# Float64 weights converted in place, and the second network's weights on GpSimd's DMA queue

## The chip, the cores and the metric

The kernel runs on one core of one Trainium2 chip. The core has a matrix engine (TensorE, PE in the profile, with its weight loads as PEld), a vector engine (VectorE, DVE), a scalar engine (ScalarE, ACT), GpSimd (POOL) and SyncE (SP), which here only issues transfers. The metric is the device time of one execution in microseconds, as the median of several runs; lower is better.

## The reference

Attention between 8 batches of 512 tokens and 32 state vectors for each of 8 heads, then two feed-forward networks on the 4352 rows that come out. All weights arrive as float64; `x` and `state` are float32, and so is the output.

```python
# x: (8, 8, 512, 64), state: (8, 8, 32, 64)
scores = scale * x @ state^T;  a  = softmax(scores);   xread = a @ state
scores2 = scale * state @ x^T; a2 = softmax(scores2);  sread = a2 @ x
x = concat([xread, sread], axis=2)      # -> rows of 512, (8 * 544, 512)
h = maximum(x @ w_in, 0)                # w_in (512, 2048)
x = (h * h) @ w_out                     # w_out (2048, 512)
a = x @ w1; b = x @ w2                  # (512, 1024) each
out = ((a * b) @ w3) @ w_out2           # w3 (1024, 1024), w_out2 (1024, 512)
```

## The kernel before

**Number format.** The kernel multiplies float32 values as pairs: `split` writes a rounded high half (a ScalarE cast, line 84) and the rest (a VectorE subtraction, line 85), and each product runs as three matmuls, high by high, low by high and high by low.

**Weights.** A float64 tile of 128x512 is loaded as pairs of int32 words (`load64`, lines 119 and 121, into a `raw` tile; there are 3 of them, and the `x` loads of lines 222 and 247 take the same ones). `convert64` makes float32 of it: `exponents` masks the exponent of the high word on VectorE (line 128) and rescales it on ScalarE (line 129); VectorE masks the mantissa (line 146), adds the low word (149), puts the sign to the exponent (152) and multiplies both (155). That is five VectorE instructions and one of ScalarE for each of 72 tiles.

**First network.** `h_tile(c, f)` makes 128 hidden features of chunk `c` (a batch; chunk 8 is the 256 state rows) in 6 matmuls, `act_h` squares the positive part and splits it into `ghl`, and `y_tile`, two tiles later, adds 12 matmuls with `w_out`'s halves into four PSUM banks (line 494). The hidden tiles need `SW`, a state times `w_in` (`make_sw`, line 426). The tiles run in a written order; `side[i]` and `late[i]` hold the attention steps and `conv()` calls that go beside tile `i`, held back behind an earlier tile's instruction by `issue_after`. A list `convs` has the order of the conversions: `w_out`'s first three tiles, `w_in`'s and `w_out`'s others, then 40 tiles of the second network (`later`: 8 of `w_out2`, 16 of `w3`, 16 of `w1` and `w2`). Each `conv()` converts one tile and starts the load of the one three places on. A `later` tile is stored as float32 in a DRAM scratch (line 214) and read back when the second network begins. Every transfer is issued by SyncE. Within these rules a scheduler sets the order on each engine when the kernel is built, and each engine then works through its list in order.

**Start.** Chunk 0 must have its attention and the first columns of `w_in` (`make_win0`, two halves by two) before its tiles run; columns 256 to 511 (`make_win0(1, 0)` and `(1, 1)`) come with tile 0, then `make_sw` for them, and tiles 2 and 3 wait for it.

**Between the networks.** `w3 @ w_out2` is multiplied out once: `load_wo2` and `load_w3` (line 641) bring the scratch back into `wst2` tiles, `w3_xpose` turns a 128x1024 row block of `w3` by 8 transposes on TensorE (line 692) into a PSUM bank, and splits it into `w3T`; `w34_rows` (line 707) multiplies it with `w_out2`'s halves in 24 matmuls. There are 8 row blocks. Beside that, `make_w` (lines 742 to 770) and `make_pair` (line 784) prepare the operands of the second network, whose matmuls (`quad`, `ab9`, `out_tile`) fill the rest of the time.

## Time and profile before

| what | value |
|---|---|
| median of 3 runs | 1258.58 us (1257.23 to 1260.12) |
| profiled execution, its own time | 1257.84 us |
| span of that execution's instructions | 1256.1 us |
| mean granted TensorE clock | 0.999 |
| instructions | 17499 |
| busy: PE, DVE, ACT, POOL | 1235.1, 789.0, 659.3, 33.5 us |
| moved by DMA | 143.23 MB, mean 114 GB/s |

Durations in the rows come from the one profiled execution, whose own time is 0.74 us under the median. A start-to-start distance of two instructions of an engine can be less than the duration shown, because the next one begins before the end of the last is recorded.

### The profile page before, as it was taken

Reading aid. Unit: us, or ns where it says so; the run is one execution under the profiler, and the core shown is the slowest. Engines: PE = TensorE matmul, PEld = TensorE weight load, DVE = VectorE, ACT = ScalarE, POOL = GpSimd, SP = SyncE. Lnnn points to the kernel's source line nnn. Section 1 sums busy time; section 2 is a strip of 40 time slices with the busy share of each in tenths; the row PEclk is TensorE's granted clock in tenths of the full one; section 3 lists DMA queues with packets and bytes.
Section 4 is the critical chain, followed back from the end, with each engine's and each line's share of the span. In section 5 each row is a group of like instructions: output and inputs, shape, how many; then the busy total and the mean of one; then the engine's idle time right before and its main releaser. Section 6 shows DMA issues by size and latency. Waiting matters only on the chain.

```text
span 1256.1 us, 17499 instructions
## 1 busy us (share of the span) xinstructions
PE 1235.1 (98%) x6672; PEld 982.1 (78%) x6672; DVE 789.0 (63%) x1403; ACT 659.3 (52%) x1188; POOL 33.5 (3%) x30
## 2 busy tenths in 40 slices
PE   6999999999999999999999999999999999999998
PEld 4667777777777777777799888888888888887886
DVE  6998778677585867742435835555655647474753
ACT  5687768666575756645655434444443524242430
POOL 0000000000000000000000000001500010000000
PEclk9999999999999999999999999999999999999999
DMA  6264646462634535201313520313430521423213
GB/s 218 69 207 145 173 129 201 113 184 82 156 130 86 190 76 173 89 18 34 134 42 111 201 76 9 120 48 126 143 134 9 201 76 52 149 74 128 76 59 117
DMA packets 125268, 143.23 MB, mean 114 GB/s; under 512 B 71680, under 2 KB 75264, under 8 KB 124672
## 3 DMA queue, kind: packets, MB, share of 16 engines
q1 hardware_dynamic: 125184, 142.11, 36.5%
q8 instruction: 52, 0.85, 0.3%
q14 instruction: 32, 0.26, 0.1%
HBM read 96.47 MB, written 45.61 MB: 113 GB/s over the span
## 4 chain that ended last, share of the span: by engine, by line
PE 93%; DMA 2%; ACT 2%; DVE 2%; issue 1%; SPq 0%; ACTq 0%; DVEq 0%
PE y L494 29%; PE po L903 14%; PE qa L822 10%; PE qd L822 7%; PE qc L822 3%; PE ps_w L707 3%; PE qe L822 3%; PE ps_sw L426 3%; PE ab L877 2%; DMA x<-in_x_dram 1%; PE ps_w L692 1%; PE ps_a L364 1%; PE ps_r L372 0%; PE ps_s L295 0%; DMA out_dram<-o 0%
## 5 line engine op out<-in xcount | busy, mean ns | idle before, releaser
L494 PE MATMUL y<-ghl,wo 128*128 128x512 f32 (+1 forms) x1728 | 403.0, 381 | 0.6 <-ACT wo L84 0.5
L494 PEld LDWEIGHTS y<-ghl,wo 128*128 128x128 f32 x1728 | 309.1, 188 | 88.4 <-ACT r L442 12.6
L85 DVE TENSOR_TENSOR ghl<-r,ghl 128x512 fp32r<-128x512 f32 (+1 forms) x144 | 95.0, 660 | 170.1 <-ACT ghl L84 167.4
L822 PE MATMUL qa<-yq,wq 128*128 128x512 f32 x576 | 146.3, 390 | 1.4 <-ACT s L830 1.4
L830 ACT COPY s<-qa 128x512 f32<-128x512 f32 x96 | 56.2, 589 | 143.7 <-PE qa L822 131.2
L822 PEld LDWEIGHTS qa<-yq,wq 128*128 128x128 f32 x576 | 107.5, 188 | 25.5 <-ACT s L830 2.4
L822 PE MATMUL qd<-yq,wq 128*128 128x512 f32 x384 | 98.4, 390 | 0.0
L903 PE MATMUL po<-w34b,c 128*128 128x512 f32 x408 | 95.8, 391 | 0.3 <-DVE o L912 0.3
L903 PE MATMUL po<-w,c 128*128 128x512 f32 x408 | 95.5, 391 | 0.0
L903 PEld LDWEIGHTS po<-w34b,c 128*128 128x128 f32 x408 | 75.7, 188 | 18.0 <-DVE c L85 1.0
L903 PEld LDWEIGHTS po<-w,c 128*128 128x128 f32 x408 | 75.5, 188 | 17.7 <-ACT o L909 1.1
L444 ACT ACTIVATE r<-r 128x512 f32<-128x512 f32 (+1 forms) x144 | 87.5, 608 | 2.9
L84 ACT CAST ghl<-r 128x512 fp32r<-128x512 f32 (+1 forms) x144 | 86.0, 597 | 3.5
L822 PEld LDWEIGHTS qd<-yq,wq 128*128 128x128 f32 x384 | 71.8, 188 | 15.7 <-ACT s L830 0.9
L129 ACT ACTIVATE ce<-ce,ebias 128x512 int32<-128x512 int32 x72 | 52.3, 727 | 44.3 <-DVE ce L128 44.3
L834 DVE TENSOR_TENSOR s<-qa,s 128x512 f32<-128x512 f32 x32 | 22.1, 692 | 75.0 <-ACT s L830 75.0
L780 POOL TENSOR_TENSOR yraw<-yraw,yp 128x512 f32<-128x512 f32 x24 | 32.8, 1373 | 987.9 <-DMA yraw<-yscr 815.2
L84 ACT CAST c<-s 128x512 fp32r<-128x512 f32 x64 | 39.7, 622 | 37.1 <-DVE s L851 36.1
L84 ACT CAST yq<-yraw 128x512 fp32r<-128x512 f32 x70 | 42.6, 622 | 24.1 <-DVE yraw L797 15.5
L912 DVE TENSOR_TENSOR o<-po,opart 128x512 f32<-128x512 f32 x34 | 23.3, 689 | 47.1 <-PE po L903 37.6
L152 DVE SCALAR_TENSOR_TENSOR ce<-raw,ce 128x512 int32<-128x512 int32 x72 | 49.3, 685 | 1.7 <-ACT ce L129 1.7
L85 DVE TENSOR_TENSOR yq<-yraw,yq 128x512 fp32r<-128x512 f32 x70 | 46.8, 684 | 5.0 <-ACT yq L84 4.7
(551 smaller groups left out, 1806.6 us busy)
## 6 DMA issues: line engine op xcount, KB each, us to landing
raw<-in_moe_w_dram SPq DMA_DIRECT2D x32, 512.0 KB, 4.3
yraw<-yscr SPq DMA_DIRECT2D x56, 256.0 KB, 5.5
yscr<-yo SPq DMA_DIRECT2D x52, 256.0 KB, 2.6
raw<-in_moe_w_out_dram SPq DMA_DIRECT2D x24, 512.0 KB, 3.9
oscr<-o SPq DMA_DIRECT2D x34, 256.0 KB, 2.2
opart<-oscr SPq DMA_DIRECT2D x34, 256.0 KB, 2.9
out_dram<-o SPq DMA_DIRECT2D x32, 256.0 KB, 2.9
raw<-in_moe_w_in_dram SPq DMA_DIRECT2D x12, 512.0 KB, 3.9
```

The source lines that it names most:

```text
L84: nc.scalar.copy(hi, src)
L85: return nc.vector.tensor_tensor(out=lo, in0=src, in1=f32(hi), op=ALU.subtract)
L129: nc.scalar.activation(e, e, ACTF.Relu, bias=ebias, scale=8.0)
L152: nc.vector.scalar_tensor_tensor(out=e, in0=hw, scalar=-(2**31), in1=e, op0=ALU.bitwise_and, op1=ALU.bitwise_or)
L426: mm = nc.tensor.matmul(pss[r][k * NS:(k + 1) * NS, cols], stT[rows, b, k, :], win_t[fg][rows, k, cols], start=True, stop=True, tile_posit ...
L444: nc.scalar.activation(r[:, :n], r[:, :n], ACTF.Square)
L494: nc.tensor.matmul(y_ps[c, d][:, :n], wo_t[f][:, wi, d * P:(d + 1) * P], t[:, gi, :n], start=(f == f0 and k == 0), stop=(f == f1 - 1 and k ...
L707: nc.tensor.matmul(ps, t[:, wi, (j % 4) * P:(j % 4 + 1) * P], wo2_t[j][:, vi, :], start=(j == 0 and k == 0), stop=(j == N1 - 1 and k == 2),)
L780: nc.gpsimd.tensor_tensor(out=t[:, n], in0=t[:, n], in1=p, op=ALU.add)
L822: nc.tensor.matmul(ps, W[w, kt][:, wi, m * P:(m + 1) * P], Y[v, kt][:, vi, :], start=(first and kt == 0 and k == 0), stop=(last and kt == ...
L830: nc.scalar.copy(t, ps)
L903: nc.tensor.matmul(ps, v[:, vi, t * P:(t + 1) * P], w[:, wi, :], start=(m == 0 and k == 0), stop=(m == QM - 1 and k == 2),)
```

## The change

The conversion is rewritten. The high word, read as a float32, is multiplied by 2^-112 straight into the output; the output's bits are shifted left by 3; the sign is put back from the high word; and the low word, scaled by 2^-29 to an integer, is added to the bits. These are four VectorE instructions, each working on what the one before it wrote. The scaled low word is made in place in the `raw` tile (in a `cw` tile for the four `win0` tiles): on ScalarE for 13 tiles (the four of `win0`, `w_out`'s tile 0 and the first 8 of `convs`), on VectorE for the other 59. The tiles `ce` and `cm` go, `cw` gets 2 buffers in place of 1, `raw` 4 in place of 3. The loads and stores of the 40 `later` tiles are issued by GpSimd in place of SyncE. A `w3` tile is loaded in four transfers of 32 partitions and turned after its conversion by one VectorE transpose, which works in blocks of 32x32; the scratch of `w_out2` becomes one tensor, read back in 16 transfers in place of 4 so that its rows match the block order. `w3_xpose` is replaced by `w3_split`, which splits `w3` out of the `wst2` tile, without TensorE or PSUM.

```diff
...
@@ -107,54 +107,46 @@
 
         if early:
             return wpool.tile([P, 512, 2], I32, tag="wo", bufs=NF, name=name)
-        return att.tile([P, 512, 2], I32, tag="raw", bufs=3, name=name)
-
-    def load64(key, src, early=False):
+        return att.tile([P, 512, 2], I32, tag="raw", bufs=4, name=name)
+
+    def load64(key, src, early=False, queue=nc.sync):
 
         t = raw_tile(early)
         flat = t.rearrange("p a b -> p (a b)")
         if isinstance(src, list):
             n = 1024 // len(src)
             for i, a in enumerate(src):
-                nc.sync.dma_start(flat[:, i * n:(i + 1) * n], a.bitcast(I32))
+                queue.dma_start(flat[:, i * n:(i + 1) * n], a.bitcast(I32))
         else:
-            nc.sync.dma_start(flat, src.bitcast(I32))
+            queue.dma_start(flat, src.bitcast(I32))
         raws[key] = t
 
-    exps = {}
-
-    def exponents(key, t):
-        e = att.tile([P, 512], I32, tag="ce", bufs=2, name="ce")
-        nc.vector.tensor_single_scalar(e, t[:, :, 1], 0x7FF00000, op=ALU.bitwise_and)
-        nc.scalar.activation(e, e, ACTF.Relu, bias=ebias, scale=8.0)
-        exps[key] = e
+    lows = {}
+
+    def low_words(key, t, scalar=True):
+        r, lw = t[:, :, 0], t[:, :, 0].bitcast(U32)
+        if key[0] == "win0":
+            r = att.tile([P, 512], I32, tag="cw", bufs=2, name="cl")
+        if scalar:
+            nc.scalar.activation(r, lw, ACTF.Copy, scale=2.0**-29)
+        else:
+            nc.vector.tensor_single_scalar(r, lw, 2.0**-29, op=ALU.mult)
+        lows[key] = r
 
     def convert64(key, out):
 
-
         t = raws.pop(key)
-        hw, lw = t[:, :, 1], t[:, :, 0].bitcast(U32)
+        if key not in lows:
+            low_words(key, t, key[0] == "win0" or key in early_keys)
+        hw, r, m = t[:, :, 1], lows.pop(key), out.bitcast(I32)
         if len(out.shape) == 3:
-            n = out.shape[2]
-            hw, lw = (v.rearrange("p (k n) -> p k n", n=n) for v in (hw, lw))
-        if key not in exps:
-            exponents(key, t)
-        e = exps.pop(key)
-        m = att.tile([P, 512], I32, tag="cm", bufs=1, name="cm")
-        if len(out.shape) == 3:
-            e, m = (v.rearrange("p (k n) -> p k n", n=n) for v in (e, m))
-        nc.vector.tensor_scalar(
-            out=m, in0=hw, scalar1=0xFFFFF, scalar2=0x100000, op0=ALU.bitwise_and, op1=ALU.bitwise_or
+            hw, r = (v.rearrange("p (k n) -> p k n", n=out.shape[2]) for v in (hw, r))
+        nc.vector.tensor_single_scalar(out, f32(hw), 2.0**-112, op=ALU.mult)
+        nc.vector.tensor_single_scalar(m, m, 3, op=ALU.logical_shift_left)
+        nc.vector.scalar_tensor_tensor(
+            out=m, in0=hw, scalar=-(2**31), in1=m, op0=ALU.bitwise_and, op1=ALU.bitwise_or
         )
-        nc.vector.scalar_tensor_tensor(
-            out=f32(m), in0=lw, scalar=2.0**-32, in1=m, op0=ALU.mult, op1=ALU.add
-        )
-        nc.vector.scalar_tensor_tensor(
-            out=e, in0=hw, scalar=-(2**31), in1=e, op0=ALU.bitwise_and, op1=ALU.bitwise_or
-        )
-        nc.vector.scalar_tensor_tensor(
-            out=out, in0=f32(m), scalar=2.0**-20, in1=f32(e), op0=ALU.mult, op1=ALU.mult
-        )
+        nc.vector.tensor_tensor(out=m, in0=m, in1=r, op=ALU.add)
 
     def load_win(fg, k):
         load64(("win", fg, k), w_in[k * P:(k + 1) * P, fg * 512:(fg + 1) * 512])
@@ -184,7 +176,7 @@
             open_splits.pop(0)()
 
     def make_wout(f):
-        w = att.tile([P, 512], F32, tag="cw", bufs=1, name="cw")
+        w = att.tile([P, 512], F32, tag="cw", bufs=2, name="cw")
         convert64(("wo", f), w)
 
         def halves():
@@ -194,24 +186,39 @@
 
         open_splits.append(halves)
 
-    w3_s = [dram.tile([P, 2, 512], F32, name=f"w3s{i}") for i in range(N1)]
+    w3_s = dram.tile([P, 4 * N1, 256], F32, name="w3s")
     w12_s = [[dram.tile([P, 2, 512], F32, name=f"w12s{i}_{k}") for k in range(ND)] for i in range(2)]
-    wo2_s = [dram.tile([P, 2, 512], F32, name=f"wo2s{i}") for i in range(N1 // 2)]
-    later = [(wo2_s[j // 2][:, j % 2, :], w_out2[j * P:(j + 1) * P, :]) for j in range(N1)]
-    for src, dst in ((w3, w3_s), (w1, w12_s[0]), (w2, w12_s[1])):
+    wo2_s = dram.tile([D1, DM], F32, name="wo2s")
+    later = [(wo2_s[j * P:(j + 1) * P, :], w_out2[j * P:(j + 1) * P, :]) for j in range(N1)]
+    w3_v = w3.rearrange("(i d q) (a c) -> i a q d c", d=2, q=NS, a=4)
+    later += [(w3_s[:, 2 * i:2 * i + 2], [w3_v[i, a] for a in range(4)]) for i in range(2 * N1)]
+    for src, dst in ((w1, w12_s[0]), (w2, w12_s[1])):
         later += [
             (dst[k][:, h, :], src[k * P:(k + 1) * P, h * 512:(h + 1) * 512])
             for k in range(src.shape[0] // P) for h in range(2)
         ]
 
+    turned = range(N1, N1 + 2 * N1)
+
     def load_later(i):
-        if i < len(later):
-            load64(("later", i), later[i][1])
+        if i not in turned:
+            if i < len(later):
+                load64(("later", i), later[i][1], queue=nc.gpsimd)
+            return
+        t = raws["later", i] = raw_tile(False)
+        for q, a in enumerate(later[i][1]):
+            nc.gpsimd.dma_start(
+                t[q * NS:(q + 1) * NS].rearrange("p (d c) k -> p d (c k)", d=2), a.bitcast(I32)
+            )
 
     def make_later(i):
-        w = att.tile([P, 512], F32, tag="cw", bufs=1, name="cw")
+        w = att.tile([P, 512], F32, tag="cw", bufs=2, name="cw")
         convert64(("later", i), w)
-        nc.sync.dma_start(later[i][0], w)
+        if i in turned:
+            m, w = w, att.tile([P, 512], F32, tag="cw", bufs=2, name="cw")
+            nc.vector.transpose(out=w, in_=m)
+            w = w.rearrange("p (d c) -> p d c", d=2)
+        nc.gpsimd.dma_start(later[i][0], w)
 
     stT = att.tile([P, B, HG, NS], F32, name="stT")
     x9T = pa.tile([P, ND, NT9], F32, tag="x9", name="x9T")
...
@@ -570,6 +577,7 @@
     convs += [("win", 3, k) for k in range(ND)] + [("wo", f) for f in range(10, NF)]
     convs += [("later", i) for i in range(len(later))]
     convs = [("wo", f) for f in range(1, 4)] + convs
+    early_keys = [("wo", 0), *convs[:8]]
     pos = [0, 0]
 
     def load_next():
@@ -584,10 +592,10 @@
         close_splits()
         k, k1 = (convs[i] if i < len(convs) else None for i in (pos[1], pos[1] + 1))
         pos[1] += 1
-        if k and k not in exps:
-            exponents(k, raws[k])
-        if k1:
-            exponents(k1, raws[k1])
+        if k in early_keys and k not in lows:
+            low_words(k, raws[k])
+        if k1 in early_keys:
+            low_words(k1, raws[k1])
         if k:
             {"wo": make_wout, "win": make_win, "later": make_later}[k[0]](*k[1:])
             load_next()
@@ -642,7 +650,10 @@
         stage[key] = t
 
     def load_wo2(i):
-        load_stage(("wo2", i), wo2_s[i])
+        t = stage["wo2", i] = w34p.tile([P, 2, 512], F32, tag="wst2", bufs=4, name="wst2")
+        rows = wo2_s.rearrange("(a k p) e -> a p k e", a=4, p=NS)
+        for a in range(4):
+            nc.sync.dma_start(t[a * NS:(a + 1) * NS], rows[a, :, 2 * i:2 * i + 2, :])
 
     def split_wo2(j):
         t = w34p.tile([P, 2, DM], F32R, tag="wo2", bufs=N1, name="wo2")
@@ -650,7 +661,7 @@
         wo2_t[j] = t
 
     def load_w3(kk):
-        load_stage(("w3", kk), w3_s[kk])
+        load_stage(("w3", kk), w3_s[:, 4 * kk:4 * kk + 4].rearrange("p (h d) c -> p h (d c)", h=2))
 
     order = [(c, f) for f0 in (0, 4) for c in range(2) for f in range(f0, f0 + 4)]
     order += [(2, f) for f in range(8)] + [(c, f) for c in range(3) for f in range(8, NF)]
@@ -685,16 +696,12 @@
 
     w3T = {}
 
-    def w3_xpose(kk):
+    def w3_split(kk):
+        src = stage["w3", kk].rearrange("p h (d k q) -> p k (h d) q", d=2, q=NS)
         for half in range(2):
-            ps = bank_m("ps_w3")
-            for j in range(4):
-                nc.tensor.transpose(
-                    ps[:, j * P:(j + 1) * P], stage["w3", kk][:, half, j * P:(j + 1) * P], ident
-                )
-            t = pa.tile([P, 2, 512], F32R, tag=f"sw{half}", bufs=2, name="w3T")
-            split(t[:, HI], t[:, LO], ps)
-            w3T[kk, half] = t
+            t = pa.tile([P, 2, 4, 4, NS], F32R, tag=f"sw{half}", bufs=2, name="w3T")
+            split(t[:, HI], t[:, LO], src[:, 4 * half:4 * half + 4])
+            w3T[kk, half] = t.rearrange("p s k d q -> p s (k d q)")
 
     w34_t = {}
     w34_s = [dram.tile([P, 2, 2, DM], F32, name=f"w34s{i}") for i in range(N1 // 4)]
@@ -922,13 +929,13 @@
 
 
     rows = list(range(N1 // 2, N1)) + list(range(N1 // 2))
-    w3_xpose(rows[0])
+    w3_split(rows[0])
     while pend:
         y_tile(*pend.pop(0))
     raw = load_w(0)
     for i, kk in enumerate(rows):
         if i + 1 < N1:
-            w3_xpose(rows[i + 1])
+            w3_split(rows[i + 1])
         if i + 4 < N1:
             load_w3(rows[i + 4])
         w34_rows(kk)
```

## Rows read from the trace of the kernel before

**Rows 1.** Part 1 of the page: busy us (share) xinstructions of each engine.
```profile
PE 1235.1 (98%) x6672; PEld 982.1 (78%) x6672; DVE 789.0 (63%) x1403; ACT 659.3 (52%) x1188; POOL 33.5 (3%) x30
```

**Rows 2.** Part 4 of the page: the chain that ended last, shares.
```profile
PE 93%; DMA 2%; ACT 2%; DVE 2%; issue 1%; SPq 0%; ACTq 0%; DVEq 0%
```

**Rows 3.** Windows: stretch, its us, busy us (instructions), PEclk, DMA share, GB/s.
```profile
23.00:34.00 11.00, 6.68 (x36) 3.98 (x37) 9.86 (x22) 8.63 (x18) 0.00 (x0) 0.91 0.42 143
34.00:100.00 66.00, 62.58 (x453) 42.71 (x452) 59.60 (x126) 51.33 (x97) 0.00 (x0) 0.99 0.43 144
100.00:680.00 580.00, 579.91 (x3444) 453.26 (x3443) 368.87 (x690) 363.69 (x652) 0.00 (x0) 1.00 0.41 119
680.00:734.00 54.00, 54.00 (x286) 46.06 (x285) 39.82 (x66) 26.64 (x52) 0.00 (x0) 1.00 0.43 147
```

**Rows 4.** The chain in time, 640 to 740 us: start, us, what.
```profile
680.38 0.87 PE ps_w L692 x8
...
690.46 0.87 PE ps_w L692 x8
...
722.13 0.87 PE ps_w L692 x8
723.00 10.91 PE ps_w L707 x48
```

**Rows 5.** Timeline, 698 to 750 us.
```profile
700.17 5.44 SPq L776 DMA_DIRECT2D yraw<-yscr  x8
...
719.88 0.68 DVE L797 TENSOR_TENSOR yraw<-yraw 128x512 f32<-128x512 f32 x1
```

**Rows 6.** Groups by line: busy us, mean ns, then idle before, releasers.
```profile
L129 ACT ACTIVATE ce<-ce,ebias 128x512 int32<-128x512 int32 x72 | 52.3, 727 | 44.3 <-DVE ce L128 44.3
...
L149 DVE SCALAR_TENSOR_TENSOR cm<-raw,cm 128x512 f32<-128x512 uint32 x72 | 49.2, 683 | 0.4
...
L128 DVE TENSOR_SCALAR ce<-raw 128x512 int32<-128x512 int32 x72 | 30.2, 420 | 4.7 <-DMA raw<-in_moe_w_in_dram 2.3 <-DMA raw<-in_moe_w_out_dram 1.8 <-DVE rs L313 0.3
...
L257 DVE STREAM_TRANSPOSE xT<-xb 128x512 f32<-128x512 f32 x20 | 14.0, 702 | 0.0
```

**Rows 7.** Timeline of VectorE, 119 to 122 us: start, us, what.
```profile
119.62 0.42 DVE L146 TENSOR_SCALAR cm<-raw 128x512 int32<-128x512 int32 x1
119.96 0.68 DVE L152 SCALAR_TENSOR_TENSOR ce<-raw,ce 128x512 int32<-128x512 int32 x1
120.56 0.68 DVE L149 SCALAR_TENSOR_TENSOR cm<-raw,cm 128x512 f32<-128x512 uint32 x1
121.28 0.69 DVE L155 SCALAR_TENSOR_TENSOR win<-cm,ce 128x512 f32<-128x512 f32 x1
```

**Rows 8.** The chain in order of time, 0 to 45 us.
```profile
24.61 0.42 DVE ce L128
...
31.24 0.61 DVE win L155
...
31.89 1.13 PE ps_sw L426 x8
```

**Rows 9.** Timeline of all engines, 0 to 36 us.
```profile
26.17 0.71 ACT L129 ACTIVATE ce<-ce,ebias 128x512 int32<-128x512 int32 x1
...
31.16 1.81 PE L426 MATMUL ps_sw<-win,stT 64*32 64x256 f32 x12 [1.08 <-ACT xT L287]
```

**Rows 10.** The chain in order of time, 45 to 110 us.
```profile
47.93 3.98 DMA x<-in_x_dram
...
66.69 4.43 DMA raw<-in_moe_w_out_dram
```

**Rows 11.** Windows, 31 to 36 us, columns as above.
```profile
31.00:36.00 5.00, 4.28 (x21) 2.25 (x22) 4.17 (x12) 1.99 (x5) 0.00 (x0) 0.66 0.00 0
```

**Rows 12.** Tile raw: count, issue ns min/median/max, first and last start us.
```profile
L121 SPq DMA_DIRECT2D raw<-in_moe_w_dram x32: 327/333/939, 247.8 to 518.3; - x32
```

**Rows 13.** Groups by line, GpSimd's costliest.
```profile
L780 POOL TENSOR_TENSOR yraw<-yraw,yp 128x512 f32<-128x512 f32 x24 | 32.8, 1373 | 987.9 <-DMA yraw<-yscr 815.2 <-DMA yp<-yscr 124.3 <-DMA oscr<-o 48.0
```

More of the change, by code (lines that the diff above doesn't have):

```diff
@@ L68 @@
     make_identity(nc, ident)
-    ebias = const.tile([P, 1], F32, name="ebias")
-    nc.vector.memset(ebias, -896.0 * 2.0**23)
+    zero = const.tile([P, 1], F32, name="zero")
+    nc.vector.memset(zero, 0.0)
     def bank_m(name):
@@ L528 @@
     warm = const.tile([P, 1], F32, name="warm")
-    nc.scalar.activation(warm, ebias, ACTF.Exp, scale=0.0)
+    nc.scalar.activation(warm, zero, ACTF.Exp, scale=0.0)
     for g in range(G):
```

## The prediction

> **What bounds the kernel now.** I read the busy shares first, then the chain, then windows by stage. The busy shares [rows 1] say that TensorE is busy nearly all the span and that VectorE, ScalarE and GpSimd are not; but they are averages over stages. The chain [rows 2] says the same by another way: 93% of it runs through TensorE. The windows [rows 3] show where the remainder lies. From 100 to 680 us TensorE is busy 579.91 of 580 us, and from 680 to 734 us all of 54. From 23 to 34 us it is busy 6.68 of 11, from 34 to 100 us 62.58 of 66, and there VectorE is busy 9.86 of 11 and 59.60 of 66. So time can be won in two ways: by taking work from TensorE, anywhere, or by relieving VectorE and the loads in the first 100 us. Everything that the change does to VectorE, ScalarE or the queues after 100 us counts for nothing unless it makes TensorE wait.
>
> **TensorE's work: the transposes of `w3`.** `w3_xpose` is on TensorE's chain 8 times, 8 instructions each, at 0.87 us; three of the 8, the last among them, stand in [rows 4]. Between them TensorE runs the products without a gap: the last two row blocks, with no transposes between them, take 10.91 us, 5.46 each. `w3_split` uses no TensorE. Gain: 8 x 0.87 = 6.98 us (7 us).
>
> Does something else fill the hole? The casts and subtractions of `w3T` stay, as many as before and of the same size; ScalarE is busy 26.64 of 54 us in this stage and VectorE 39.82 [rows 3]. Seven us shorter, VectorE would be busy 39.82 of 47. What is late next is VectorE's work on the first pair: its operands are asked for at 700.17, when the work on `w1` and `w2` lets their tiles go, and its last instruction that needs no tile of `w3T` ends at 719.88 + 0.68 = 720.56 [rows 5]. TensorE leaves the stage at 723.00 + 10.91 = 733.91 [rows 4], and would at 726.9. That leaves 6.4 us. One more row block's splits moved in front of it cost three instructions of about 0.68 us, 2.0. So I take the full 6.98; if the cover is gone, part of it.
>
> **VectorE's work: the conversion.** Before, five instructions: two of the form of line 128 at 0.420 us and three of the form of line 149 at 0.683 [rows 6], 2.89 us. After: two single-input and two two-input instructions, 2.21 us, and for 59 tiles a third single-input one, 2.63. No row shows the multiply, the shift or the low word in place; the nearest is line 128, single-input, reading every other word and writing int32, and I take its price for all three. Durations overlap, though. Instructions on VectorE start 0.34 us after a 0.42 one and 0.60 after a 0.68 one, but 0.72 after it where the second needs the first's result (line 155 behind 149) [rows 7]. The new four each need the one before. Run alone, they cost 0.46 + 0.46 + 0.72 + 0.69 = 2.33 us, against 0.34 + 0.34 + 0.60 + 0.72 + 0.69 = 2.69 before: a saving of 0.36 for the 13 early tiles and about none for the 59. With other instructions between them it is up to 0.68 and 0.26. In the 580 us after 100 us, where VectorE is busy 368.87 [rows 3], this is hidden, and so are the 16 new block transposes at 0.702 [rows 6], 11.2 us in all, which is also what they would cost with no idle time to hide in. ScalarE loses 72 instructions of 0.727 us [rows 6] and gains 13, which I price alike: 59 x 0.727 = 42.9 us less, hidden too, by TensorE.
>
> **The start, 24 to 32 us.** Tiles 2 and 3 wait for `make_sw` on columns 256 to 511, and that for two conversions that VectorE works on from 24.61 to 31.85 us [rows 8]. They save 2 x (0.36 to 0.68), and line 128 of the next tile, 0.34, leaves their midst: 1.0 to 1.7 us. But TensorE's second half of `ps_sw` starts at 31.16, after a wait for ScalarE, and only then stops for the conversion until 31.89 [rows 8, 9]. ScalarE has two of line 129 in front, the second at 26.17 [rows 9]; the new low words need only the loaded tile and may run earlier. If they don't, 0.7 us is won; if they do, 1.7. I take 1.2.
>
> **The start, 34 to 100 us.** Nine early tiles save 3.2 to 6.1 us of VectorE's 59.60. The fourth `raw` tile lets a load start one conversion sooner; the chain has two such loads, of 3.98 and 4.43 us [rows 10]. Not all of this reaches the end, since the chain here hops between TensorE, ScalarE, VectorE and transfers. At most TensorE's idle time goes, 66 - 62.58 = 3.42 us, and with it the spell from 31 to 36 us in which its granted clock is 0.66 on average, part of it at the lower level of 1.2 GHz, behind the gap before `ps_sw` [rows 11]; that costs (1 - 0.66) x 5 = 1.7 us. Together 5.1. At least: the order on the engines is made anew, and a second such spell would cost 1.7. So -1.7 to 5.1; I take 1.8, half of the smaller VectorE saving and a little for the loads.
>
> **The queues.** SyncE loses 40 loads and 40 stores at 0.33 us [rows 12], which nothing waited for after 100 us, and gains 12 issues for `w_out2`, 12 x 0.33 = 4 us while TensorE is fully busy. GpSimd has no arithmetic until the second network, and takes 8 + 16 x 4 + 16 loads and 40 stores. In the program's order a load stands behind the store of the tile converted just before; that store waits for VectorE, as it did on SyncE. On before, 32 of these loads are issued between 247.8 and 518.3 us, 270.5 / 31 = 8.73 us apart [rows 12], and each is made three conversions ahead. A load of 4.43 us [rows 10] fits in that many times.
>
> No row shows a transfer issued by GpSimd, so its price has ends: SyncE's 0.33 us an issue below [rows 12], an arithmetic instruction of GpSimd at 1.373 above [rows 13]. Four loads and a store for a `w3` tile are then 1.6 to 6.9 us, under 8.73, so I cost the move at nothing. The Trainium skill (SBUF — State Buffer, sections "SBUF: two separate sides" and "Who interferes with whom") advises against it: GpSimd writes the descriptors of its own transfers and cannot while VectorE runs a two-port instruction, and it gives 620 ns for such a transfer alone and about 3100 ns under a VectorE copy. By that, 2.5 us more for each of five transfers is 12.4 us for each `w3` tile, and the kernel would become some 16 x (12.4 - 8.73) = 59 us slower; this is an estimate from that page. Nothing here can say whether it holds, but the single-input instructions of line 128 last only 0.42 us [rows 6].
>
> **Sum.** 6.98 + 1.2 + 1.8 = 9.98 us less. The profiled execution took 1257.84 us; it becomes 1247.86. It lay 0.74 us under the median of the three runs, so for the median 1248.6 us.
>
> **The rivals.**
> - *The start gives more:* VectorE is the only bound there, both idle times close (11 - 6.68 = 4.32 and 3.42) and the slow spell goes: 6.98 + 4.32 + 5.1 = 16.4 us, 1242.2. For it, VectorE's 59.60 of 66; against it, the waits for ScalarE and loads.
> - *VectorE binds between the networks:* half of the transposes' time comes back as a wait for the pair's splits, and the start gives nothing: 3.5 us, 1255. It needs VectorE's work there to end 6.4 us later, where I find 2.0.
> - *The change doesn't do what it says:* the new order at the start loses what the transposes give, 7 us, for instance by a late load or two such as those on the chain now [rows 10]: 1256 to 1261, no change.
> - *GpSimd's queue becomes the bound, and the kernel is slower:* VectorE takes its list in order, so a conversion without its tile holds up the `ghl` splits behind it, and two tiles later TensorE. It decides when four loads and a store take over 8.73 us, 1.75 each. At 2.0 each the 16 `w3` tiles cost 16 x 1.27 = 20 us: 1269. For it, the price is unseen; against it, that is above even GpSimd's 1.373 [rows 13].
>
> **How the numbers follow.** The forecast, with its ends 6.98 + 0.7 - 1.7 = 6.0 and 6.98 + 1.7 + 5.1 = 13.8 (1244.8 to 1252.6): 0.68. More at the start (1242.2 to 1244.8): 0.07. VectorE bound between the networks (1252.6 to 1256): 0.13. No change, within 0.2% or 2.5 us, about what a measurement of this kernel can tell: 0.06. Slower: 0.06. The range 1242 to 1254 holds the first two and half of the third, 0.81. Faster 0.88, same 0.06, slower 0.06.
>
> **What would show it.** No instruction on TensorE between the row blocks, each 5.46 us after the last, and this stage 7 us shorter with `ab` following as soon as now; the second `ps_sw` starting at 30 to 31 us; TensorE's idle time from 34 to 100 us 1 to 3 us less; single-input VectorE instructions near 0.42 us; TensorE still at 580 of 580 afterwards. I am wrong if row blocks wait for splits, if conversions wait for loads on GpSimd's queue, or if the multiply or the low word costs VectorE 0.68 us at the start.

## The result, and the profile of the changed kernel

The changed kernel takes 1244.7 us (median of 5 runs, 1242.08 to 1245.63), the kernel before 1258.15 (5 runs). The ratio is 0.9887, interval 0.9875 to 0.9898: 13.45 us less, where 9.98 were forecast. The span of the profiled execution went from 1256.1 to 1242.7 us.

The busy shares (part 1 of the page; before: [rows 1]) and the chain's shares (part 4; [rows 2]) keep their shape. TensorE has 64 instructions less, the transposes of `w3`; ScalarE, VectorE and GpSimd matter no more than before.

```profile
PE 1226.2 (99%) x6608; PEld 977.0 (79%) x6608; DVE 780.8 (63%) x1406; ACT 623.9 (50%) x1129; POOL 102.9 (8%) x158
...
PE 94%; DMA 2%; DVE 2%; ACT 1%; SPq 1%; issue 0%; DVEq 0%
```

The windows by stage (columns as in [rows 3]; the two last stages moved with the work, and the last line is the spell of [rows 11]):

```profile
23.00:34.00 11.00, 8.94 (x43) 5.88 (x44) 9.57 (x23) 8.09 (x17) 0.00 (x0) 0.79 0.53 191
34.00:100.00 66.00, 64.82 (x469) 45.91 (x468) 55.30 (x121) 52.01 (x98) 0.00 (x0) 0.98 0.43 144
100.00:667.00 567.00, 567.00 (x3362) 442.44 (x3361) 362.25 (x695) 323.70 (x582) 70.02 (x128) 1.00 0.43 120
667.00:720.00 53.00, 53.00 (x277) 45.65 (x276) 41.64 (x69) 29.84 (x59) 0.00 (x0) 1.00 0.46 156
31.00:36.00 5.00, 5.00 (x15) 3.80 (x12) 4.21 (x12) 3.54 (x8) 0.00 (x0) 0.50 0.01 2
```

TensorE's idle time is 2.06 us in the first stage (before 4.32) and 1.18 in the second (3.42). Its granted clock, though, is lower: 0.50 throughout from 31 to 36 us, where it was 0.66 on average. Between the networks, the chain in order of time (before: [rows 4]):

```profile
673.17 4.33 PE y L501 x36
677.50 43.56 PE ps_w L714 x192
...
724.59 11.17 PE ab L884 x91
```

The 8 row blocks are one piece, 192 matmuls in 43.56 us, 5.45 a block, with nothing between them. On the chain `ab` follows 3.5 us behind the end of that piece, as it did before; in these 3.5 us TensorE runs 12 `qa` matmuls and, from 723.60 on, the first of `ab` (before: 736.45).

VectorE's and ScalarE's prices (groups by line; before: [rows 6]). The integer addition of line 149 appears as a custom operation on halves of 16 bits:

```profile
L146 DVE SCALAR_TENSOR_TENSOR cw<-raw,cw 128x512 int32<-128x512 int32 x56 | 38.4, 685 | 1.2
L149 DVE CUSTOM_DVE_ANT_0 cw<-raw,cw 128x1024 uint16<-128x1024 uint16 x56 | 38.0, 679 | 0.7
L210 POOL DMA_DIRECT2D raw<-in_moe_w_dram x64 | 34.4, 544 | 42.8 <-DVE cw L149 25.0 <-DVE xT L264 17.3 <-issue 0.2
L133 DVE TENSOR_SCALAR raw<-raw 128x512 int32<-128x512 uint32 x59 | 24.6, 417 | 0.0
L144 DVE TENSOR_SCALAR cw<-raw 128x512 f32<-128x512 f32 x56 | 23.4, 419 | 0.0
...
L219 DVE STREAM_TRANSPOSE cw<-cw 128x512 f32<-128x512 f32 x16 | 11.3, 707 | 0.3
...
L221 POOL DMA_DIRECT2D w3s<-cw x16 | 9.3, 579 | 55.8 <-DVE cw L219 54.2 <-DVE nm L315 1.4 <-issue 0.2
...
L131 ACT ACTIVATE raw<-raw 128x512 int32<-128x512 uint32 x9 | 6.1, 692 | 0.2 <-DMA raw<-in_moe_w_in_dram 0.2
```

Where the 13.4 us of the two spans came from is seen best in the starts of the 144 hidden tiles, that is of each tile's first `ph` matmul in the timeline of TensorE. These are the starts in the kernel before, and by how much the other kernels are earlier (-) or later; the experiments below are in the table already.

| hidden tile | before, us | changed | conv_alone | raw3 | on_sync | x_on_gp | turn_alone | turn_gp |
|---|---|---|---|---|---|---|---|---|
| 2 | 33.42 | -2.3 | -2.9 | -3.2 | -2.7 | -2.9 | +0.8 | +0.1 |
| 6 | 64.10 | -1.1 | -2.3 | -2.5 | -2.3 | -3.6 | +1.4 | +0.5 |
| 12 | 100.44 | -4.7 | -5.8 | -4.8 | -5.9 | -7.1 | +1.6 | +0.6 |
| 30 | 183.35 | -4.6 | -5.7 | -4.7 | -5.8 | -7.1 | +1.6 | +0.6 |
| 66 | 350.48 | -5.1 | -6.2 | -4.8 | -6.3 | -7.6 | +0.2 | +0.9 |
| 84 | 432.77 | -5.3 | -6.4 | -5.0 | +0.3 | -7.9 | +13.8 | +1.2 |
| 102 | 516.91 | -5.8 | -6.8 | -5.4 | -0.4 | -8.3 | +15.0 | +1.2 |
| 138 | 662.93 | -5.8 | -6.8 | -5.5 | -0.4 | -8.3 | +15.0 | +1.2 |

So the changed kernel wins 4.7 us by tile 12, 1.1 more in five steps of 0.23 to 0.25 between tile 30 and tile 102, and 7.1 from tile 138 to `ab` (12.85 in all there, 736.45 to 723.60).

### The profile page after: what moved, and what is told of

Its sections match the earlier page's. It is cut to its first block, busy times and chain, and to the rows that moved or that the text cites. A ratio compares the mean times of both kernels' runs of the same rounds, so it can differ in the third digit from the quotient of the medians.

```text
span 1242.7 us, 17483 instructions
## 1 busy us (share of the span) xinstructions
PE 1226.2 (99%) x6608; PEld 977.0 (79%) x6608; DVE 780.8 (63%) x1406; ACT 623.9 (50%) x1129; POOL 102.9 (8%) x158
## 3 DMA queue, kind: packets, MB, share of 16 engines
q1 hardware_dynamic: 114368, 110.65, 29.6%
## 4 chain that ended last, share of the span: by engine, by line
PE 94%; DMA 2%; DVE 2%; ACT 1%; SPq 1%; issue 0%; DVEq 0%
PE y L501 30%; PE po L910 13%; PE qa L829 10%; PE qd L829 7%; PE ps_w L714 4%; PE qc L829 3%; PE qe L829 3%; PE ps_sw L433 3%; PE ab L884 2%; DMA x<-in_x_dram 1%; PE ps_s L302 1%; DMA out_dram<-o 1%; DVE yq L85 1%; PE ps_r L379 1%; PE ps_a L371 1%; DMA st<-in_state_dram 0%
## 5 line engine op out<-in xcount | busy, mean ns | idle before, releaser
L85 DVE TENSOR_TENSOR c<-s,c 128x512 fp32r<-128x512 f32 x64 | 48.3, 773 | 2.1
L829 PE MATMUL qc<-yq,wq 128*128 128x512 f32 x192 | 49.5, 390 | 0.0
L829 PE MATMUL qe<-yq,wq 128*128 128x512 f32 x192 | 49.2, 389 | 0.0
```

Source lines behind the costliest of these rows:

```text
L85: return nc.vector.tensor_tensor(out=lo, in0=src, in1=f32(hi), op=ALU.subtract)
L829: nc.tensor.matmul(ps, W[w, kt][:, wi, m * P:(m + 1) * P], Y[v, kt][:, vi, :], start=(first and kt == 0 and k == 0), stop=(last and kt == ...
```

## The experiments

The kernel before, timed beside them, took 1258.45 us (first four, 9 runs), 1258.25 (next four, 9 runs) and 1258.13 (last three, 7 runs).

**turn_alone: only `w3` turned on VectorE.** The kernel before with the new `w3` path: loads in four parts, transpose on VectorE, `w3_split`, the new scratch of `w_out2`. SyncE's queue and the old conversion stay.

```diff
 def make_later(i):
     w = att.tile([P, 512], F32, tag="cw", bufs=1, name="cw")
     convert64(("later", i), w)
+    if i in turned:
+        m, w = w, att.tile([P, 512], F32, tag="cm", bufs=1, name="cm")
+        nc.vector.transpose(out=w, in_=m)
+        w = w.rearrange("p (d c) -> p d c", d=2)
     nc.sync.dma_start(later[i][0], w)
```

> The kernel before with the turning of w3 alone: blocks on VectorE after the conversion, w3_split in place of w3_xpose, SyncE's queue and the old conversion kept. Theory (the transposes' TensorE time comes back whole, 8 x 0.87 us): 7.0 us under the kernel before, ratio 0.9944, and the start as before. Rival (VectorE binds between the networks): 3 to 4 us under, row blocks with gaps between them. If this gives more than 8 us, the two parts don't add up as I have them.

Measured: 1266.44 us (1265.95 to 1267.37), ratio 1.0065 [1.0053, 1.0078]. Taking 7 us of work from TensorE made the kernel 8 us slower, against both theories. The table says where: 15 us go between hidden tiles 66 and 102, while `w3` is converted in the first network. The window from 400 to 500 us of this kernel, which is fully busy in the kernel before (99.97 of 100), has holes:

```profile
400.00:500.00 100.00, 96.14 (x533) 71.05 (x532) 65.73 (x126) 55.38 (x98) 0.00 (x0) 0.98 0.54 140
```

TensorE did 533 matmuls there against 588. The busy time alone hides most of the loss; the count shows it. Part of it is the clock's: 0.98 in this window, because the granted clock was at its lower level of 1.2 GHz for 3.4 us from 448.6, behind three waits of TensorE of 0.7 to 1.4 us.

**conv_alone: only the conversion.** The kernel before with the new `convert64`, 4 `raw` and 2 `cw` tiles; `w3` on TensorE, SyncE's queue. The diff is against the changed kernel, whose old parts come back with it.

```diff
-        nc.gpsimd.dma_start(later[i][0], w)
+        nc.sync.dma_start(later[i][0], w)
...
-    w3_split(rows[0])
+    w3_xpose(rows[0])
```

> The kernel before with the new conversion alone: four raw tiles and two cw tiles, w3 turned by TensorE and all transfers on SyncE as before. Theory (the start is worth what the transposes don't explain, 13.4 - 7.0): 5.5 to 6.5 us under the kernel before, ratio 0.995, all of it won by 110 us into the span. Rival (my sum, 3.0 us from the start, and the rest from GpSimd's queue): 3 us under, 0.9976.

Measured: 1250.54 us (1249.45 to 1252.88), ratio 0.9940 [0.9928, 0.9953]: 7.9 us less, more than either expectation. 6.8 us of it are there by tile 102, 5.8 by tile 12. The conversion and its tiles are thus worth about as much as the transposes' 7.0.

**raw3: the changed kernel with 3 `raw` tiles.**

```diff
-        return att.tile([P, 512, 2], I32, tag="raw", bufs=4, name=name)
+        return att.tile([P, 512, 2], I32, tag="raw", bufs=3, name=name)
```

> The changed kernel with three raw tiles in place of four. Theory (the relief of VectorE makes the start's gain, the loads little): 0 to 1 us over the changed kernel, 13 us under the kernel before. Rival (the fourth raw tile makes most of what I sized too small): 2.5 to 4 us over the changed kernel, some 10 us under the kernel before, with waits for raw tiles on the chain near 48 and 67 us again.

Measured: 1246.36 us (1243.5 to 1247.14), ratio 0.9898 [0.9883, 0.9912]; the intervals of this and the changed kernel overlap. The trace has what the times can't settle: two loads on the chain again, where the changed kernel and conv_alone have none there (the chain in order of time, 45 to 102 us; before: [rows 10]):

```profile
50.09 4.94 DMA raw<-in_moe_w_in_dram
...
60.78 3.85 DMA raw<-in_moe_w_in_dram
```

Against conv_alone, whose granted clock fell for as long at 30 to 35 us, raw3 is 1.0 us later at tile 12 (-4.8 against -5.8). The fourth `raw` tile is worth about 1 us, together with the order that comes with it: with 3 tiles the scheduler puts TensorE's matmuls into another order from the first tiles on.

**on_sync: the changed kernel with the `later` tiles' loads and stores on SyncE.**

```diff
-                load64(("later", i), later[i][1], queue=nc.gpsimd)
+                load64(("later", i), later[i][1], queue=nc.sync)
...
-            nc.gpsimd.dma_start(
+            nc.sync.dma_start(
...
-        nc.gpsimd.dma_start(later[i][0], w)
+        nc.sync.dma_start(later[i][0], w)
```

> The changed kernel with the loads and stores of the second network's weights issued by SyncE as before. Theory (the queue is hidden either way): within 1 us of the changed kernel. Rival (SyncE's queue, freed of 80 transfers, is what gives time after 110 us): 1 to 3 us over the changed kernel. Rival from the Trainium skill (GpSimd's transfers are held up under VectorE's two-port instructions): under the changed kernel.

Measured: 1249.64 us (1249.1 to 1251.18), ratio 0.9934 [0.9921, 0.9946], some 5 us slower than the changed kernel, which refutes the theory. Up to tile 66 the two run alike but for the clock; then on_sync loses 5 to 6 us by tile 90. The timeline of SyncE's queue shows what is late (start, us, what; a long duration of an issue means that it waited):

```profile
390.69 9.05 SPq L254 DMA_DIRECT2D xb<-in_x_dram  x16
399.84 0.43 SPq L221 DMA_DIRECT2D w3s<-cw  x1
400.37 14.34 SPq L121 DMA_DIRECT2D raw<-in_moe_w_dram  x2
428.44 0.33 SPq L221 DMA_DIRECT2D w3s<-cw  x1
...
429.31 0.44 SPq L269 DMA_DIRECT2D X<-in_x_dram  x1
```

And the same loads of `xb` and `X` in the changed kernel, where SyncE issues nothing of `w3`:

```profile
366.49 13.37 SPq L254 DMA_DIRECT2D xb<-in_x_dram  x16
382.75 4.32 SPq L269 DMA_DIRECT2D X<-in_x_dram  x2
```

`xb` comes 24 us later and `X` 47 us. From 380 to 480 us SyncE waited 27.8 us for VectorE's transposes, to be able to store, and 17.5 us for a `raw` tile (its waits by what was waited for):

```profile
SPq L221 <- DVE cw L219: 27.8, 4, 13.6
SPq L121 <- DVE xT L264: 17.5, 2, 13.6
```

The batch's attention, which needs `xb` and `X`, is then late for the hidden tiles that use it. VectorE in turn once stands still for a store on this queue (timeline of VectorE; the idle time and its cause in brackets):

```profile
449.17 0.43 DVE L144 TENSOR_SCALAR cw<-raw 128x512 f32<-128x512 f32 x1 [0.29 <-DMA w12s<-cw]
```

From the start of tile 78 to that of tile 102 both kernels run the same 637 matmuls (the windows add one at the edge), first on_sync and then the changed kernel:

```profile
400.78:516.48 115.70, 114.57 (x638) 84.00 (x637) 80.51 (x166) 64.10 (x113) 0.00 (x0) 1.00 0.55 153
400.50:511.15 110.65, 110.65 (x638) 83.87 (x637) 75.88 (x154) 63.47 (x113) 12.87 (x24) 1.00 0.43 124
```

Of the 5.05 us only 1.13 are idle time of TensorE. In on_sync the scheduler has set some of the batch's `ps_s` between `y` matmuls, in fours; four take as long there as 16 in one piece in the changed kernel (second line):

```profile
426.04 1.05 PE L302 MATMUL ps_s<-xT,stT 64*32 64x512 f32 x4
412.84 1.09 PE L302 MATMUL ps_s<-xT,stT 64*32 64x512 f32 x16
```

This gave a new theory, tested by the next two and by x_on_gp: the queue costs nothing by itself, but `w3`'s loads and stores, put into one list with the loads of `x`, hold these up.

**turn_gp: turn_alone with the `later` tiles on GpSimd's queue.** The lines of on_sync, the other way round, in turn_alone (`load64` gets its argument as in the change).

```diff
-        nc.sync.dma_start(later[i][0], w)
+        nc.gpsimd.dma_start(later[i][0], w)
```

> The kernel before with w3 turned on VectorE (as in turn_alone: old conversion, three raw tiles, the turned tile written into cm and stored from there), but with the loads and stores of the 40 later tiles issued by GpSimd in place of SyncE. Theory: what made turn_alone 8 us slower is SyncE's queue, in which the loads of the next batches' x stand behind w3's stores and small loads, which wait for VectorE and for a raw tile; with those on GpSimd's queue only the transposes' 7.0 us are left, so 1251.5 (1250.5 to 1252.8). Rival: the cm tile, held by the store after each of 16 turns, stops VectorE's next conversion whatever queue issues the store; then it stays at 1264 to 1267. A mixture would lie between, at 1255 to 1262.

Measured: 1253.91 us (1252.4 to 1254.57), ratio 0.9962 [0.9949, 0.9974]. Of turn_alone's loss 12.5 us are gone by the queue alone, and the 15 us between tiles 66 and 102 are 0.3 (table). The theory's range was missed by 1.1 us: this kernel is 1.2 us later than before at tile 138, half of it from before 64 us, where its granted clock is low earlier and longer than in the kernel before, and half in two steps of 0.27 at tiles 54 and 70 (see "After 100 us" below). The tile `cm`, held by the store, is not the cause. TensorE's list up to the end of the first network is the one of the kernel before, and turn_alone's is not.

**no_turn: the changed kernel with `w3` on TensorE.** GpSimd's queue and the new conversion stay: conv_alone but for the queue.

```diff
-    w3_split(rows[0])
+    w3_xpose(rows[0])
```

> The changed kernel with w3 transposed on TensorE as before (whole loads of w3 and w_out2's old scratch), GpSimd's queue and the new conversion kept: conv_alone with the other queue. Theory: the queue matters only because w3's four-part loads and late stores stand before the x loads; without the turn there is nothing to stand behind, so the time is conv_alone's, 1250.5 (1249.5 to 1251.7). Rival: GpSimd's queue is worth its 5 us by itself, as on_sync against the changed kernel would suggest; then 1245.5 (1244.5 to 1247).

Measured: 1251.84 us (1249.95 to 1252.52), ratio 0.9945 [0.9932, 0.9958], against conv_alone's 1250.54. Without the turn GpSimd's queue wins nothing, as the theory says and the rival denies; TensorE's list is the same in both. Against the changed kernel it also gives the worth of turning `w3` when the queue is GpSimd's: 7.1 us.

**x_on_gp: on_sync with the loads of `x` on GpSimd instead.** The two queues are swapped.

```diff
-                    nc.sync.dma_start(
+                    nc.gpsimd.dma_start(
                         t[p0:p0 + NS, k * 512:(k + 1) * 512].rearrange("p (c i) -> p c i", i=NS),
...
-        nc.sync.dma_start(t, x[b, g * HG:(g + 1) * HG].rearrange("h (j p) d -> p h j d", p=P))
+        nc.gpsimd.dma_start(t, x[b, g * HG:(g + 1) * HG].rearrange("h (j p) d -> p h j d", p=P))
```

> on_sync (the changed kernel with the loads and stores of the later tiles on SyncE) with the loads of x that run beside the first network (xb and X, lines 254 and 269) issued by GpSimd: the two queues are swapped. Theory: on_sync lost its 5 us because those x loads stood in SyncE's queue behind w3's stores and loads (X 47 us later than in the changed kernel); any queue of their own frees them, so the time is the changed kernel's, 1244.7 (1243.5 to 1246). Rival: the loss is in the later tiles' transfers themselves, issued by SyncE beside the y stores; then it stays at on_sync's 1249.6 (1248.5 to 1251).

Measured: 1242.96 us (1242.52 to 1243.72), ratio 0.9882 [0.9867, 0.9897]. on_sync's loss is gone although `w3` is still on SyncE. `X` is loaded in time again (timeline of GpSimd, the idle time before and its end in brackets):

```profile
364.22 5.14 POOL L254 DMA_DIRECT2D xb<-in_x_dram  x8 [55.36 <-DVE cw L149]
...
380.43 2.31 POOL L269 DMA_DIRECT2D X<-in_x_dram  x2 [2.19 <-PE ps_r L379]
```

TensorE's list of instructions is the same, one by one, in this kernel and the changed one, while on_sync's differs from both, above all between 413 and 444 us: the order is made when the kernel is built, and with `w3` and `x` in one queue it has `ps_s` and `ps_sw` behind other tiles. So the loss has two parts. 1.13 us are recorded as waiting; in the rest the order has a share, and the broken-up `ps_s` is one item of it. How large that share is, the runs do not separate.

**lows_dve: the first nine low words on VectorE.** The changed kernel; `win0`'s four stay on ScalarE.

```diff
-            low_words(key, t, key[0] == "win0" or key in early_keys)
+            low_words(key, t, key[0] == "win0")
...
-    early_keys = [("wo", 0), *convs[:8]]
+    early_keys = []
```

> The changed kernel with the low words of the first nine tiles (w_out's tile 0 and eight of convs) made on VectorE in place of ScalarE; the four of win0 stay on ScalarE. Takes 9 x 0.68 = 6.1 us from ScalarE, gives VectorE 9 x 0.417 = 3.8 us, most of it before 60 us. Theory: VectorE's shorter conversions made the start's gain, and it is still what the first tiles wait for; then 1246.5 (1245.5 to 1248.5). Rival: ScalarE with 52 us of 66 in 34 to 100 us has become what the first tiles wait for; then 1243 (1241.5 to 1244).

Measured: 1243.45 us (1242.6 to 1245.34), ratio 0.9881 [0.9863, 0.9898]: no difference from the changed kernel that these runs can tell. Three of its four runs had a granted clock of 1.0, so the 1.2 us by which its median is lower need not be ScalarE's; keep_lows takes this up.

**keep, keep8: filling a gap of TensorE ahead of the fall of its clock.** Idle 128x128 matmuls before the second `ps_sw` group; their result is not used. 14 in keep, 8 in keep8.

```diff
+    def keep(n):
+        t = bank_y(3, "idle")
+        for _ in range(n):
+            nc.tensor.matmul(t[:, :P], ident, ident, start=True, stop=True)
+
-    side[1] = [*xp1, lambda: make_sw(0, 0, slice(256, 512)), lambda: make_wout(0), a2t[0], s2[1], sc1]
+    side[1] = [*xp1, lambda: keep(14), lambda: make_sw(0, 0, slice(256, 512)), lambda: make_wout(0), a2t[0], s2[1], sc1]
```

> The changed kernel with 14 idle 128x128 matmuls (some 1.5 us at 0.107) in TensorE's gap of 1.9 us before the second ps_sw group, at 27.2 to 29.1 us; their result is not used. Theory: the granted clock, at 1.2 GHz from 29.5 to 36.4 us in the changed kernel's profile, falls because of the gaps ahead of it, and filling this one keeps it at 2.4 GHz or shortens the fall: 1 to 3.4 us less, 1242.5 (1241 to 1243.7). Rival: the fall comes anyway, as it came in the kernel before and in the other runs at 30 to 36 us; then 1244.7 (1243.7 to 1245.7).

Measured: 1242.39 us (1242.02 to 1242.66), ratio 0.9871 [0.9858, 0.9885], as the theory said. In all four runs the granted clock is 0.999 or 1.0 over the span, where the changed kernel's five runs have 0.995 to 1.0, and lows_dve and x_on_gp, with the gap left open, 0.998 to 1.0 and 0.995 to 1.0. The window of the slow spell, first in the changed kernel and then in keep (the number behind the five busy times is PEclk):

```profile
29.00:37.00 8.00, 7.86 (x33) 5.04 (x34) 6.42 (x18) 5.49 (x13) 0.00 (x0) 0.57 0.05 21
```

```profile
29.00:37.00 8.00, 7.13 (x57) 3.65 (x56) 7.97 (x23) 7.92 (x18) 0.00 (x0) 1.00 0.07 27
```

The spell is gone in keep. It was not in every execution with the gap open either, as x_on_gp's profile shows further on, so keep shows a steadier clock rather than a cause. The idle matmuls took longer than I had reckoned, 3.29 us (28 records, two for each), and put `ps_sw` at 29.97 us, 0.8 later than in the changed kernel. Hence keep8:

> keep with 8 idle matmuls in place of 14. In keep's trace the 14 took 3.29 us and put the second ps_sw group 0.8 us later than in the changed kernel; 8 should take 1.9 us, the gap itself. Theory: the clock holds as in keep and the 0.8 us comes back: 1241.7 (1241 to 1242.6). Rival: with the shorter filling the clock falls in some runs as in the changed kernel, and the median is 1243 to 1245.

Measured: 1243.85 us (1243.08 to 1245.83), ratio 0.9891 [0.9876, 0.9905]. The clock held at the start (1.00; 0.998 to 1.0 over the span), and hidden tiles came early, but the time didn't: in its profiled execution, the slowest of the four, TensorE lost 3.2 us from 900 to 1200 us, all of it in `qa` and `qd` waiting for ScalarE's `s`, and behind the longest of these waits, 2.2 us before 1067.96, the granted clock was at the lower level for 3.4 us from 1068.6. That is neither theory, and it lies far behind the start.

**keep_lows: keep8 with the low words as in lows_dve.**

```diff
-    early_keys = [("wo", 0), *convs[:8]]
+    early_keys = []
...
+    side[1] = [*xp1, lambda: keep(8), lambda: make_sw(0, 0, slice(256, 512)), lambda: make_wout(0), a2t[0], s2[1], sc1]
```

> keep8 with the low words of the first nine tiles on VectorE, as in lows_dve, which ended 1.2 us below the changed kernel with its clock at 1.0 in three of four runs. Theory: that difference was the clock's and not ScalarE's, so with the clock held there is nothing to gain or lose: keep8's time, 1241.7 (1240.7 to 1243). Rival: ScalarE did pace the start, and 1 us more comes off: 1240.5.

Measured: 1245.04 us (1243.88 to 1247.02), ratio 0.9902 [0.9886, 0.9919]. No gain: it lies above the theory's range and overlaps with keep8. The starts of the tiles, which lie before the second network and its differences, say the same: at tile 12, in four profiles without a slow spell, keep8 is 7.5 us ahead of the kernel before and keep_lows 7.2, x_on_gp and lows_dve both 7.1. So the rival falls: the early low words on ScalarE do not pace the start.

keep and x_on_gp are at 1242.4 and 1243.0 the best that was run. Their intervals overlap with the changed kernel's, and keep's tight runs are the only sign that it is better. Its profile does not put this down to the start: keep comes to its first `ab` at 722.0 us, later than x_on_gp (721.0) and keep8 (720.8), and is ahead because its second network takes 518.2 us from there, against 520.0 and 523.3.

## Why the prediction was right, and where its sizes were off

**The transposes: right, and the size too.** Predicted 6.98 us. From the last `y` matmul to the last row block: before 684.12 to 733.91, 49.8 us; after 677.50 to 721.06, 43.6; that is 6.2, and the first transposes lay ahead of that stretch, 0.87 more. no_turn against the changed kernel gives 7.1. VectorE did not bind between the networks: 41.64 of 53 us, and no wait between row blocks.

**24 to 32 us: taken at 1.2, measured 2.3.** Tile 2 starts 2.3 us earlier, in the three kernels with the same TensorE list up to there and the clock at full speed 2.7 to 2.9 (no_turn, conv_alone, x_on_gp). I had reckoned that TensorE could not start the second half of `ps_sw` before 31.16, since it waited for ScalarE [rows 9]. That was misread: this `ps_sw`, 16 records, begins at 29.45, goes on at 31.16 behind ScalarE's second copy of `xT` (30.52), and its last eight weights load at 31.89 behind the conversion. Now these three are at 29.14, 29.49 and 30.15 (the weight loads of the last eight, before and changed):

```profile
31.89 0.20 PEld L426 LDWEIGHTS ps_sw<-win,stT 64*32 64x32 f32 x8 [0.59 <-DVE win L155]
30.15 0.20 PEld L433 LDWEIGHTS ps_sw<-win,stT 64*32 64x32 f32 x8 [0.47 <-ACT xT L294]
```

ScalarE's copies come earlier, the first by 0.3 us and the second by 1.0, for two reasons. Its two instructions of line 129 are gone from in front of them: their successors run at 14.90 and 16.36, 9 to 10 us before VectorE converts these tiles. And in the new order the exponential that stood before the second copy (line 311, at 29.80) comes behind it (31.70). From the timeline of the changed kernel:

```profile
14.90 0.66 ACT L131 ACTIVATE cl<-raw 128x512 int32<-128x512 uint32 x1 [0.81 <-DMA raw<-in_moe_w_in_dram]
...
16.36 0.68 ACT L131 ACTIVATE cl<-raw 128x512 int32<-128x512 uint32 x1 [0.80 <-DVE mx L336]
...
25.01 0.75 DVE L144 TENSOR_SCALAR win<-raw 128x512 f32<-128x512 f32 x2
...
28.76 0.68 DVE L149 CUSTOM_DVE_ANT_0 win<-win,cl 128x1024 uint16<-128x1024 uint16 x1
```

The two conversions go hand in hand, so no instruction waits for the one before it, and the pair takes 25.01 to 29.44, 4.4 us in place of the 7.2 of [rows 8]. Part of that, too, is the order: between them VectorE now has one instruction of other work, the `ghl` subtraction at 28.16, where it had two of `ghl`, one of `nm` and line 128 of the next tile.

**34 to 100 us: taken at 1.8, measured 2.2 to 2.9, with a slow spell in it.** TensorE's idle time fell by 3.42 - 1.18 = 2.24 us; from tile 2 to tile 12 the changed kernel wins 2.4, conv_alone, whose slow spell is as long as the one before, 2.9, and x_on_gp, which has none, 4.2. The single prices were right (0.42 and 0.68 us; the low word in place 0.417), about 1 us of it is the fourth `raw` tile (raw3), and the choice of engine for the early low words makes no difference (keep_lows).

**After 100 us: forecast nothing, measured 1.1.** This step failed, by a little. At five places the kernel before loses 0.23 to 0.25 us each, with a conversion that "is hidden". At one, ahead of tile 35, the weights of a `y` matmul wait until ScalarE has copied the last group out of PSUM; ScalarE had an instruction of line 129 shortly before (199.02). Before (timeline of PEld), and the same loads in the changed kernel, without a wait:

```profile
203.61 2.61 PEld L494 LDWEIGHTS y<-ghl,wo 128*128 128x128 f32 x12 [0.35 <-ACT yo L504]
```

```profile
198.68 2.68 PEld L501 LDWEIGHTS y<-ghl,wo 128*128 128x128 f32 x12
```

At the other four, just ahead of tiles 54, 70, 86 and 102, it is the attention's `ps_a` that waits, and for VectorE: the subtraction of line 85 must first have read `ps_sw` out of the PSUM bank. Before, two instructions of a conversion (lines 128 and 146) stand in front of that subtraction; in the changed kernel it follows the one of `ghl` at once, and the conversion comes after (timelines of VectorE and PEld, at tile 54; before, then changed):

```profile
292.69 0.42 DVE L128 TENSOR_SCALAR ce<-raw 128x512 int32<-128x512 int32 x1
293.03 0.42 DVE L146 TENSOR_SCALAR cm<-raw 128x512 int32<-128x512 int32 x1
293.37 1.28 DVE L85 TENSOR_TENSOR sw<-ps_sw,sw 128x512 fp32r<-128x512 f32 x2
...
294.10 0.42 PEld L364 LDWEIGHTS ps_a<-ident,e 128*128 128x128 f32 x4 [0.44 <-DVE sw L85]
```

```profile
288.20 1.28 DVE L85 TENSOR_TENSOR sw<-ps_sw,sw 128x512 fp32r<-128x512 f32 x2
...
288.94 0.46 PEld L371 LDWEIGHTS ps_a<-ident,e 128*128 128x128 f32 x4 [0.17 <-DVE sw L85]
```

TensorE counts as all but fully busy in both, which is why [rows 3] don't show it. conv_alone has the whole gain; turn_gp, with the old conversion, has none of it, and where it loses 0.27 us at tile 54 the same wait is 0.72 us. ScalarE's cast, which the subtraction needs, starts only 0.6 us before it (292.74), so what VectorE's order alone is worth there was not shown.

**The clock: against the forecast.** I counted the spell of [rows 11] as a possible gain and a second one as a possible loss of 1.7 us. The second came: in the changed kernel's profile the clock is at 1.2 GHz for 3.4 us from 12.3 and for 6.8 us from 29.4, together 10.2 in place of 3.41 us (from 31.9). x_on_gp has the same list on TensorE and no such spell; its window is

```profile
29.00:37.00 8.00, 7.82 (x52) 3.89 (x52) 7.63 (x22) 7.81 (x17) 0.00 (x0) 1.00 0.03 10
```

with 52 matmuls where the changed kernel ran 33, and at tile 12 it is 2.45 us ahead (93.30 against 95.75). With a spell about as long as the kernel before had, the start gives 5.8 us (conv_alone), with none 7.1, and here it gave 4.7.

**The queues: the price was right, the worth was missed.** A GpSimd issue takes 0.53 to 0.59 us, near the lower end of 0.33 to 1.373; four loads and a store for a `w3` tile are 2.8 us, far under 8.73. Its transfers land nearly like SyncE's (part 6 of the page: median times to landing at the end):

```profile
raw<-in_moe_w_dram POOLq DMA_DIRECT2D x64, 128.0 KB, 3.4
raw<-in_moe_w_dram POOLq DMA_DIRECT2D x16, 512.0 KB, 4.3
```

In on_sync, where SyncE issues them, the same loads take 3.1 and 4.7 us:

```profile
raw<-in_moe_w_dram SPq DMA_DIRECT2D x64, 128.0 KB, 3.1
raw<-in_moe_w_dram SPq DMA_DIRECT2D x16, 512.0 KB, 4.7
```

So the rival by the Trainium skill (SBUF — State Buffer, "SBUF: two separate sides") did not come about: against the 2.5 us more for a transfer that the prediction took from that page, the small loads land 0.3 us later and the large ones 0.4 earlier, with VectorE busy 63% of the span. Which of VectorE's instructions held GpSimd up, and whether any did, no run here shows. But "costed at nothing" hid a condition. The move is worth nothing by itself (no_turn) and 5 us as soon as `w3` is turned (on_sync), 12.5 with the slower conversion (turn_alone and turn_gp). My argument that the loads find time enough looked at the moved transfers alone, and not at what stands behind them in the queue that they leave.

**The sum.** Forecast 6.98 + 1.2 + 1.8 = 9.98. Measured to `ab`: 7.1 + 2.3 + 2.4 + 1.1 = 12.9 us, and 0.5 more in the second network, too little to be told: from the first `ab` on, the thirteen profiles take 518.2 to 523.3 us for the same work. The time, 1244.7, is at the border of the likeliest case (down to 1244.8) and of the rival in which the start gives more: its mechanisms are those of the forecast, two terms of the start were taken too small, and one small term was missing. Where in the range it fell is in part luck: x_on_gp, with the same list on TensorE and no slow spell in its profile, takes 1243.0, inside that rival's range.

## What to carry to other kernels

Before a transfer is added to an in-order queue, list what is issued behind it: a store that waits for an engine delays every load after it, when the kernel runs and already in the order that the scheduler builds, and here that turned 7 us won into 8 lost until one of the two parties got another queue. An instruction taken from an engine that is far from busy, or moved in its list, can still pay, when the copy or subtraction that frees a PSUM bank stands behind it; look at the waits of the weight loads, since TensorE's busy time hardly shows them. And compare matmul counts or the starts of like tiles, not busy shares, where TensorE seems full in both kernels.

## What the runs showed of the hardware

- At the start the granted clock fell to the lower level of 1.2 GHz near 30 us in the profiled executions of seven of these kernels (among them both kernels compared) and stayed at 2.4 GHz in six: no_turn, lows_dve, x_on_gp and the three with idle matmuls. The changed kernel's five times go with its mean clock: 1242.08 us at 1.0, 1243.31 at 0.998, 1244.7 to 1245.63 at 0.995 to 0.997. Why an execution with the gap open keeps its clock stays open.
- An integer addition of two int32 tiles runs on VectorE as a custom operation on 128x1024 halves of 16 bits, at 0.68 us, like a float32 one of two inputs.
- From tile 78 to tile 102 on_sync takes 5.05 us more than the changed kernel for the same 637 matmuls, and 3.92 of them are recorded as busy (114.57 us against 110.65). The Trainium skill (Perfetto Trace Analysis, "Tensor Engine Instruction (MATMUL, LD_WEIGHTS)") says that the end of a TensorE instruction is estimated and not observed; how much of the 3.92 is a wait that such an end covers, and how much the other order of the matmuls, no run here shows.
- Four `ps_s` matmuls alone between `y` matmuls take 1.05 us, 16 in one piece 1.09 (on_sync and the changed kernel).
